# Block 0's weight and softmax steps taken off GpSimd, its list of steps made anew, and operand tiles padded to one address modulo 256 bytes

## The chip, the cores and the metric

The kernel runs on one core of one Trainium2 chip. A core has five engines with a queue of instructions each: TensorE (PE; its loads of stationary operands are shown apart as PEld), VectorE (DVE), ScalarE (ACT), GpSimd (POOL) and SyncE (SP), which only starts transfers here. Engines run beside each other and wait for each other by semaphores. The metric is the device time of one execution in microseconds, the median of the runs shown.

## The reference, cut to what matters

```python
# q, k, v: (8 batches, 8 heads, 576 tokens, 64), float32
scores = (q @ k.T) / sqrt(64)
# heads 0..3: local mask, 0 <= i - j < 32; heads 4..7: strided mask, j <= i and j % 32 == i % 32
attn = exp(scores - max) / (sum + 1e-9)
x = (attn @ v)                       # as (4608 tokens, 512)
gate = 1 / (1 + exp(-(x @ w_gate)))  # w_gate, w_val: (512, 1536), w_out: (1536, 512), float64
out = ((gate * (x @ w_val)) @ w_out).astype(float32)
```

Attention is sparse: a query of a local head sees 32 keys, a query of a strided head at most 18. Most arithmetic is in the three dense products of the gated layer, 4608 tokens by 512 by 1536.

## The kernel before, in words

**Precision.** The weights are float64 and TensorE works here on a 32-bit form (fp32r) that keeps part of the fraction. So every operand is held as two tiles, a high part and a low part (value less high part), and each dense product is issued three times: high by high, high by low, low by high. The twelve slices of the hidden dimension (f = 0 to 11) have three weights each (i = 0 gate, 1 value, 2 out); "w0_1" is slice 0's value weight. A weight reaches TensorE by seven steps: `wr` loads its 64-bit words; `wa` (L244) and `wb` (L248) turn the upper and the lower words into two tiles on ScalarE; `ws` (L252) shifts the upper on VectorE; `wd` (L256) adds the two, which gives the number in single precision; `wu` (L260) casts it to the high part; `wl` (L263) subtracts for the low part. `wd` and `wl` run on VectorE, their variants `wdp` and `wlp` on GpSimd; `wu` runs on ScalarE, its variant `wuv` on VectorE.

**Blocks.** Tokens are worked in blocks of 512: block k (0 to 7) holds the first 512 tokens of batch k, block 8 the 64 left over of each batch. For a block and a slice f, gate and value are 12 products of 512 columns each (L512: 4 pieces of the 512 inputs, 3 products each), then come the sigmoid (`s`, L520, ScalarE), gate times value (`m`, L525, VectorE), the split into hh (`x`, L532, ScalarE; variant `xv` on VectorE) and hl (`y`, L536, VectorE; variant `yp` on GpSimd), and 12 products with the out weight (`o`, L543), which add into four banks. In blocks 0 to 2 gate and value are done so. Blocks 3 and 4, 5 and 6, 7 and 8 are worked in pairs, where half products (L770) of sums and differences of weights (made on GpSimd during blocks 0 to 2, L693 to L698, and kept in DRAM) replace them; `ring` tiles bring those weights back, `xs` tiles hold sums of x.

**Attention.** Each batch is four pairs of heads (0 and 2 local, 1 and 3 strided). A pair of batches 0 and 1 goes through load (`fQ`, `fV`), scores on TensorE (`fS`, L329), mask (`fM`), row maximum (`fA`, L353), subtraction (`fU`, L357; variant `fUp` on GpSimd), exponential (`fE`, L370, ScalarE), sum and reciprocal (`fN`, L374 to L376), multiplication (`fW`, L380; variant `fWp` on GpSimd), transposes on TensorE (`fT`), a copy to pt (`fP`), the product with v on TensorE (`fX`, L433), and the split into xh (`fH`, L469), xl (`fL`, L473) and leftovers (`fR`, L482). While block 0 is in work, the weights arrive for the first time, and batch 1's attention is done between its products.

**What sets the order.** The list ORDER names every step of the program; a program walks it and issues each step's instructions, and no scheduler moves them. So the queue of each engine is the list with the other engines' steps left out, and an instruction whose operand is late holds all behind it on its engine. `fg0.1.2` is block 0's product of slice 0, weight 1 (value), third piece of x; `wu2.0` casts weight w2_0; a p behind the letters means GpSimd, a v VectorE. BANKS says which PSUM banks some of the first steps use.

**Addresses.** Tiles come from pools ("keep", "work", "first", "odd"), where each tag takes a place of its own size behind the others; so the size of one tile moves all that lie behind it. The tiles whose size the change touches are qk (an attention pair's q and k, L283) and mx (row maxima and sums, L308).

Of the kernel before, what the change touches and what calls it, by code (L numbers as in the profile page):

```python
# [73 lines left out]
wuv2.0 fg0.1.1 fH0.3 ws1.1 wlp2.0 wu1.0 fg0.0.1 fL0.3 wb1.1 fg0.1.2 wl1.0 fR0.3 wr3.2 wb0.2 fg0.0.2 wd1.1 wa0.2 fg1.0.0 wuv1.1 wa2.1 wr4.0 fg0.0.3
wl1.1 wb2.1 ws0.2 fg1.0.1 wr4.2 ws2.1 wdp0.2 fg1.1.0 wd2.1 fg0.1.3 s0.0 wuv2.1 wu0.2 fg1.1.1 m0.0 fg2.0.0 wl0.2 x0.0 fS1.0 wl2.1 wb3.0 yp0.0 wa1.2
wb1.2 fg1.0.2 fM1.0 fQ1.1 wa3.0 fg2.1.0 wr5.0 fA1.0 wb2.2 wr5.2 fg1.1.2 wa2.2 fU1.0 fg2.0.1 wr5.1 ws3.0 fg1.0.3 wd3.0 fg1.1.3 s0.1 ws1.2 fg2.0.2 wu3.0
m0.1 wlp3.0 fg2.1.1 xv0.1 fg2.0.3 wd1.2 fE1.0 fg2.1.2 yp0.1 wuv1.2 o0.0 fN1.0 wlp1.2 s0.2 fW1.0 wa3.1 wb3.1 ws3.1 wa4.1 ws2.2 fg3.0 wdp3.1 wr6.0 wa3.2
ws4.1 wb3.2 ws3.2 wd2.2 wu3.1 wr6.1 wdp3.2 wl3.1 wu2.2 fT1.0 wb4.1 wa4.0 wd4.1 wr7.0 fg2.1.3 fP1.0 fZ1.1 wuv4.1 wlp2.2 wb4.0 o0.1 m0.2 wr6.2 wuv3.2
s0.3 ws4.0 wlp3.2 x0.2 wa4.2 y0.2 wb4.2 fg3.1 ws4.2 wlp4.1 wr7.1 wd4.2 wuv4.2 wb5.1 wl4.2 fS1.1 wb5.2 m0.3 wa5.2 xv0.3 wa5.1 o0.2 fM1.1 fQ1.2 wr8.1
wr8.0 fA1.1 y0.3 fUp1.1 wd4.0 fX1.0 ws5.1 wu4.0 ws5.2 wlp4.0 o0.3 wd5.1 fR1.0 fV1.1 wdp5.2 fE1.1 fH1.0 fN1.1 wa5.0 fg4.0 wb5.0 fL1.0 fWp1.1 wu5.1  # L80
wr7.2 ws5.0 wu5.2 wd5.0 fg4.1 wl5.2 wlp5.1 s0.4 wu5.0 wa6.1 wl5.0 ws6.1 wb6.0 fT1.1 m0.4 wa6.0 xv0.4 wb6.1 fg5.0 y0.4 fP1.1 ws6.0 wb6.2 wd6.0 wa6.2
wuv6.0 wl6.0 fS1.2 wd6.1 s0.5 wa7.0 ws6.2 wdp6.2 fg6.0 wu6.1 fM1.2 fQ1.3 wb7.0 fA1.2 wl6.1 fUp1.2 ws7.0 wb7.1 fg5.1 wuv6.2 wa7.1 wl6.2 wdp7.0 ws7.1
wd7.1 fE1.2 fX1.1 wu7.1 m0.5 fN1.2 fg6.1 fV1.2 s0.6 wuv7.0 fWp1.2 x0.5 wl7.0 fH1.1 wl7.1 fR1.1 yp0.5 fL1.1 fg7.0 wa8.1 wb8.1 ws8.1 wa8.0 wr9.0 wdp8.1
m0.6 wa7.2 xv0.6 wb7.2 o0.4 y0.6 s0.7 ws8.0 wb8.0 ws7.2 wuv8.1 wr8.2 wlp8.1 fg7.1 wdp8.0 wdp7.2 wu8.0 fT1.2 m0.7 wl8.0 x0.7 o0.5 wuv7.2 fZ1.3 wb9.0
y0.7 fP1.2 wl7.2 wa9.0 wa8.2 ws9.0 wr9.2 wb8.2 wd9.0 fg8.1 wr9.1 wuv9.0 ws8.2 wlp9.0 wdp8.2 fS1.3 wuv8.2 o0.6 fM1.3 LQ0 wlp8.2 wa9.1 wb9.1 ws9.1 fA1.3
# [856 lines left out]
```

## Time and profile before

| | before |
|---|---|
| time, median of 3 runs (lowest to highest) | 956.06 us (954.44 to 957.01) |
| the profiled execution's own time | 955.16 us |
| its span, instructions | 953.4 us, 18540 |
| PE busy | 929.7 us, 98% |
| PEld busy | 757.6 us, 79% |
| DVE busy | 608.6 us, 64% |
| ACT busy | 418.6 us, 44% |
| POOL busy | 180.7 us, 19% |
| moved by DMA | 154.14 MB, 162 GB/s |

The span runs from the first to the last instruction of one profiled execution; the time of that execution is 1.8 us longer. A share is busy time over the span, so it is an average over stages with different limits. Instructions are named by their source line, the tile that they write and those that they read ("g<-xh,w"). Matmul ends are modelled, and a product of 512 columns is shown with about 390 ns although products follow each other faster than that, so the pace is to be read from starts of products, not from the sum of durations.

### The profile page before, as it was taken

What the parts mean: (1) busy time and instruction counts of PE and PEld (TensorE: products, weight loads), DVE (VectorE), ACT (ScalarE), POOL (GpSimd) and SP (SyncE); (2) the same over time, 40 slices, a digit from 0 to 9 for tenths busy, and PEclk for the clock granted to TensorE, in tenths of its full rate; (3) what the DMA queues carried; (4) which work ended last, traced back from release to release, by engine and by line L of the source; (5) the groups of instructions that cost most, each with busy time, mean ns of one, the idle gap of its engine ahead of it and who ended that gap; (6) DMA issues with size and microseconds to landing.
All of it is one profiled execution on the core that took longest, in us unless ns stands there. A gap on an engine that the chain in (4) does not pass through costs nothing.

```text
span 953.4 us, 18540 instructions
## 1 busy us (share of the span) xinstructions
PE 929.7 (98%) x7624; PEld 757.6 (79%) x7624; DVE 608.6 (64%) x973; ACT 418.6 (44%) x759; POOL 180.7 (19%) x226
## 2 busy tenths in 40 slices
PE   5988999999999999999999999999999999999998
...
GB/s 366 313 194 81 169 96 176 119 176 197 197 121 222 232 160 189 210 185 187 173 187 175 174 68 172 194 186 144 147 163 143 23 140 193 152 147 144 64 45 44
DMA packets 90068, 154.14 MB, mean 162 GB/s; under 512 B 5888, under 2 KB 40192, under 8 KB 89984
## 3 DMA queue, kind: packets, MB, share of 16 engines
...
q8 instruction: 60, 0.98, 0.4%
...
## 4 chain that ended last, share of the span: by engine, by line
PE 85%; DVE 8%; DMA 2%; ACT 2%; SPq 1%; issue 1%; POOL 1%; DVEq 0%; ACTq 0%
PE p L770 21%; PE o L543 18%; PE d L770 15%; PE g L512 7%; PE v L512 7%; PE o_a L543 5%; PE o_g L543 3%; PE o_v L543 3%; PE x_a L433 2%; DVE high L256 1%; DVE w L263 1%; PE s_g L329 1%; PE s_v L329 1%; PE s L329 1%; PE x L433 1%
## 5 line engine op out<-in xcount | busy, mean ns | idle before, releaser
L770 PE MATMUL p<-xs,ring 128*128 128x512 f32 x864 | 204.8, 389 | 0.0
L770 PEld LDWEIGHTS p<-xs,ring 128*128 128x128 f32 x864 | 162.2, 188 | 34.1
L543 PE MATMUL o<-w,hh 128*128 128x512 f32 x576 | 183.4, 399 | 0.0
L770 PE MATMUL d<-xs,ring 128*128 128x512 f32 x648 | 155.8, 389 | 0.0
L770 PEld LDWEIGHTS d<-xs,ring 128*128 128x128 f32 x648 | 121.6, 188 | 25.2
L543 PEld LDWEIGHTS o<-w,hh 128*128 128x128 f32 x576 | 106.4, 188 | 24.9
L543 PE MATMUL o<-w,hl 128*128 128x512 f32 x288 | 113.6, 395 | 0.0
L804 DVE TENSOR_TENSOR e<-e,d 128x512 f32<-128x512 f32 x54 | 37.1, 687 | 110.4 <-PE d L770 63.3
L401 DVE STREAM_TRANSPOSE pt<-sb 32x320 f32<-32x320 f32 (+1 forms) x192 | 102.9, 536 | 3.8
L512 PE MATMUL v<-xh,w 128*128 128x512 f32 x256 | 87.8, 400 | 4.6 <-DVE t L525 2.4
L512 PE MATMUL g<-xh,w 128*128 128x512 f32 x256 | 86.7, 396 | 2.8 <-DVE sb L349 1.2
L799 ACT COPY e<-p 128x512 f32<-128x512 f32 x54 | 31.7, 588 | 118.5 <-PE p L770 118.2
L543 PEld LDWEIGHTS o<-w,hl 128*128 128x128 f32 x288 | 54.2, 188 | 12.8
L512 PEld LDWEIGHTS v<-xh,w 128*128 128x128 f32 x256 | 49.0, 192 | 16.1 <-issue 2.8
L512 PEld LDWEIGHTS g<-xh,w 128*128 128x128 f32 x256 | 48.0, 188 | 15.5 <-DVE sb L349 1.8
L698 POOL TENSOR_TENSOR sum<-sum 128x128 f32<-128x128 f32 x96 | 51.2, 536 | 6.3
L536 DVE TENSOR_TENSOR hl<-hid,hh 128x512 fp32r<-128x512 f32 x36 | 28.0, 780 | 36.5 <-ACT hh L532 36.4
L512 PE MATMUL v<-xl,w 128*128 128x512 f32 x128 | 51.0, 399 | 0.0
L512 PE MATMUL g<-xl,w 128*128 128x512 f32 x128 | 50.2, 392 | 0.0
L693 POOL TENSOR_TENSOR sum<-w 128x256 f32<-128x256 f32 x44 | 34.9, 812 | 71.1 <-DMA sets<-sum 68.6
L812 ACT ACTIVATE e<-e 128x512 f32<-128x512 f32 x54 | 34.2, 633 | 28.7 <-DVE e L804 28.4
L532 ACT CAST hh<-hid 128x512 fp32r<-128x512 f32 x36 | 22.3, 620 | 53.0 <-PE o_a L543 43.6
...
## 6 DMA issues: line engine op xcount, KB each, us to landing
...
```

The lines of the kernel that those rows point to most:

```text
L329: nc.tensor.matmul(sc[j % len(sc)][g * m : (g + 1) * m, j // len(sc) * BANK + s * kk : j // len(sc) * BANK + (s + 1) * kk], q_[d, at : at ...
L401: nc.vector.transpose(dst[to : to + LB, :, col : col + LB], src[part * LB : (part + 1) * LB, :, h * LB : (h + 1) * LB])
L433: nc.tensor.matmul(at_bank(r, (u * per + g) * m, (u * per + g + 1) * m)[j * D : (j + 1) * D], v[part][rows, slot * P + j * D : slot * P + ...
L512: nc.tensor.matmul(o, w, x, start=first and n == 0, stop=last and n == len(todo) - 1)
L536: by.tensor_tensor(hl, whole_h.pop((k, f)), hh.bitcast(F32), op=ALU.subtract)
L543: nc.tensor.matmul(acc[k][i], h[:, i * P : (i + 1) * P], w, start=f == 0 and n == 0, stop=f == NF - 1 and n == 2,)
L693: nc.gpsimd.tensor_tensor(u[:, at : at + 2], part(wh[f][i], c), part(wl[f][i], c), op=ALU.add)
L698: nc.gpsimd.tensor_tensor(u[:, to], u[:, x], u[:, y], op=op)
L770: nc.tensor.matmul(to, w[:, (wi * 2 + c) * P : (wi * 2 + c + 1) * P], x[xi][:, c], start=p in (1, 2, 5) and c == j == 0, stop=c == 1 and j ...
L799: nc.scalar.copy(x, two[m, 0])
L804: nc.vector.tensor_tensor(x, x, two[m, 1], op=ALU.add)
L812: nc.scalar.activation(x, x, AF.Sigmoid)
```

## The change

It has three parts.

1. **Steps that change engine.** In the stretch of the list that builds block 0 (up to block 1's first gate), all variants on GpSimd go: 16 `wdp`, 13 `wlp`, 5 `yp`, 6 `fUp` and 4 `fWp` become `wd`, `wl`, `y`, `fU` and `fW` on VectorE. The variants of casts on VectorE go too: 21 `wuv` and 5 `xv` become `wu` and `x` on ScalarE.
2. **The list made anew.** That stretch, and the first steps behind it, stand in another order; 2329 steps before and after, the last 1703 the same and in the same order. BANKS gives some first steps other banks.
3. **Sizes of tiles.** The qk tile grows from 1198 to 1216 words (4792 to 4864 bytes in each partition, 19 times 256), and the mx tile from 16 to 64 words (64 to 256 bytes). The two pairs of batch 0 that borrow the places of weights (HOMES) share one kept tile mxs of 64 words in place of a tile of their own each.

The diff, with the list cut to its first lines:

```diff
@@ -36,6 +36,7 @@
 SK = NG * GS + QB - GS
 SQK = SK + NG * GS
+WIDE = 64 * -(-SQK // 64)
 TB = 512
@@ -54,7 +55,7 @@
 BANKS = {
-    "S0.0": "o1", "S0.1": "o1", "T0.1": "o0", "X0.1": "o0", "T0.2": "o1", "X0.2": "o1", "S0.3": "o1", "T0.3": "o0", "g1": "o0",
+    "T0.0": "o0", "X0.0": "o0", "S0.1": "o0", "T0.1": "o1", "X0.1": "o1", "T0.2": "o0", "T0.3": "o0", "X0.3": "o0", "g1": "o0",
 }
@@ -67,105 +68,105 @@
-fQ0.1 fZ0.1 fZ0.3 C fQ0.0 fQ0.2 fV0.2 fQ0.3 fV0.1 wr0.1 fV0.0 wr0.0 fS0.1 fV0.3 wr2.0 wr1.0 wr1.1 wr0.2 fM0.1 wr2.1 wr1.2 fA0.1 fS0.0 fU0.1 fQ1.0
-fM0.0 fE0.1 fS0.2 fN0.1 fA0.0 fW0.1 fUp0.0 fM0.2 fT0.1 fA0.2 fE0.0 fS0.3 fUp0.2 fP0.1 fN0.0 fX0.1 fM0.3 fWp0.0 fE0.2 fA0.3 fR0.1 fH0.1 fN0.2 wa0.1
-fUp0.3 fT0.0 wb0.1 fW0.2 wr3.0 fP0.0 fL0.1 fT0.2 fE0.3 ws0.1 wa0.0 fN0.3 wdp0.1 fX0.0 fP0.2 wb0.0 fW0.3 wu0.1 wr2.2 fX0.2 fV1.0 ws0.0 fR0.0 fH0.0
...
+fQ0.0 fZ0.1 fZ0.3 C fQ0.2 fQ0.1 fV0.0 fQ0.3 fV0.2 fV0.1 wr0.0 fV0.3 fS0.0 wr1.0 wr0.1 wr1.1 fM0.0 fQ1.0 wr2.0 wr2.1 fA0.0 wr0.2 fS0.2 wr1.2 fU0.0
+fE0.0 fM0.2 fS0.1 fN0.0 fA0.2 fM0.1 fU0.2 fS0.3 fW0.0 fE0.2 fA0.1 fT0.0 fN0.2 fP0.0 fW0.2 fU0.1 fT0.2 fM0.3 fE0.1 fN0.1 fP0.2 wa0.0 fX0.2 wb0.0 fW0.1
+wr2.2 fA0.3 fT0.1 fH0.2 wa1.0 fU0.3 fR0.2 fX0.0 fL0.2 fE0.3 ws0.0 fP0.1 fN0.3 fR0.0 fV1.0 fH0.0 fX0.1 wa0.1 fW0.3 wb0.1 fL0.0 fH0.1 wr3.0 wd0.0 fT0.3
...
@@ -182,6 +183,7 @@
     ident = cst[:, SL * KL + GS :]
+    mxs = pool.tile([P, 64], F32, name="mxs")
     xr = {}
@@ -280,7 +282,7 @@
-            qk = space.tile([P, SQK], F32, tag="qk", name=f"qk{b}_{step}")
+            qk = space.tile([P, WIDE], F32, tag="qk", name=f"qk{b}_{step}")
@@ -305,7 +307,7 @@
-            tiles["mx"] = space.tile([P, 16], F32, tag="mx" + str(step) * bool(home), name=f"mx{b}_{step}")
+            tiles["mx"] = mxs[:, 16 * step : 16 * step + 16] if home else space.tile([P, 64], F32, tag="mx", name=f"mx{b}_{step}")
```

Lines of the changed kernel stand two lower than those of the kernel before (L263 becomes L265).

Three places show what the new list does to the queues. The first is VectorE's queue around the first weights that are finished (w is the high and low part of one weight, high and low its two word tiles, xl the low part of batch 0's x, mx and sb an attention pair's row values and scores). Before:

```order
L380 TENSOR_TENSOR sb0_3_83<-sb0_3_83,mx0_3_84 128x12x54
L252 TENSOR_SCALAR high0_0_363<-high0_0_363 128x512
L256 ISA high0_0_363<-high0_0_363,low0_0_364 128x1024
L473 TENSOR_TENSOR xl0_74<-x0_0_370,xh0_73 128x512
L260 CAST w0_0_472<-high0_0_363 128x512
L263 TENSOR_TENSOR w0_0_472<-high0_0_363,w0_0_472 128x512
L252 TENSOR_SCALAR words2_0_460<-words2_0_460 128x512
L473 TENSOR_TENSOR xl0_74<-x0_2_416,xh0_73 128x512
L252 TENSOR_SCALAR high1_0_491<-high1_0_491 128x512
L256 ISA high1_0_491<-high1_0_491,low1_0_492 128x1024
L260 CAST w2_0_525<-words2_0_460 128x512
```

And with the change:

```order
L382 TENSOR_TENSOR sb0_3_84<-sb0_3_84,mxs_62 128x12x54
L475 TENSOR_TENSOR xl0_75<-x0_0_364,xh0_74 128x512
L258 ISA high0_0_306<-high0_0_306,low0_0_307 128x1024
L254 TENSOR_SCALAR high0_1_443<-high0_1_443 128x512
L254 TENSOR_SCALAR high1_0_359<-high1_0_359 128x512
L265 TENSOR_TENSOR w0_0_465<-high0_0_306,w0_0_465 128x512
L258 ISA high0_1_443<-high0_1_443,low0_1_444 128x1024
L475 TENSOR_TENSOR xl0_75<-x0_1_414,xh0_74 128x16x18
L475 TENSOR_TENSOR xl0_75<-x0_1_414,xh0_74 128x16x12
L475 TENSOR_TENSOR xl0_75<-x0_1_414,xh0_74 128x16x2
L265 TENSOR_TENSOR w0_1_520<-high0_1_443,w0_1_520 128x512
L258 ISA high1_0_359<-high1_0_359,low1_0_360 128x1024
```

The casts (L260) have left VectorE; the adds and subtractions of w0_1, GpSimd's before, stand in the queue, and between the steps of one weight stand steps of another.

The second place is GpSimd's queue from the program's branch on (sum tiles are the sums of weights for the later blocks). Before:

```order
L938 UNCONDITIONAL_BRANCH
L310 MEMSET sb0_1_80 128x12x10
L310 MEMSET sb0_3_83 128x12x10
L357 ISA
L357 TENSOR_TENSOR sb0_0_195<-sb0_0_195,mx0_0_196 128x640
L357 TENSOR_TENSOR sb0_2_246<-sb0_2_246,mx0_2_247 128x640
L380 TENSOR_TENSOR sb0_0_195<-sb0_0_195,mx0_0_196 128x640
L357 TENSOR_TENSOR sb0_3_83<-sb0_3_83,mx0_3_84 128x12x54
L256 TENSOR_TENSOR high0_1_333<-high0_1_333,low0_1_334 128x512
L263 TENSOR_TENSOR w0_1_412<-high0_1_333,w0_1_412 128x512
L256 TENSOR_TENSOR words2_0_460<-words2_0_460 128x512
L263 TENSOR_TENSOR w2_0_525<-words2_0_460,w2_0_525 128x512
```

With the change:

```order
L940 UNCONDITIONAL_BRANCH
L312 MEMSET sb0_1_81 128x12x10
L312 MEMSET sb0_3_84 128x12x10
L312 MEMSET sb1_1_689 128x12x10
L312 MEMSET sb1_3_1364 128x12x10
L695 ISA
L695 TENSOR_TENSOR sum0_0_1_1777<-w0_0_465 128x256
```

Until the first sum of weights GpSimd now only sets four tiles to zero.

The third place is TensorE's queue around block 0's first gated product (t are transposes, x attention results, v and g products of the value and the gate weight). Before:

```order
L433 MATMUL x0_0_370<-pt0_0_348,vv0_0_105 64x32 x36
L433 MATMUL x0_2_416<-pt0_2_407,v0_2_93 64x32 x32
L433 MATMUL x0_2_416<-pt0_2_407,u0_2_95 64x32 x4
L388 MATMUL t0_3_462<-cst_61,sb0_3_83 128x128 x6
L512 MATMUL v0_0_478<-xh0_73,w0_1_412 128x512
L512 MATMUL v0_0_478<-xl0_74,w0_1_412 128x512
L512 MATMUL v0_0_478<-xh0_73,w0_1_412 128x512
L512 MATMUL g0_0_486<-xh0_73,w0_0_472 128x512
```

With the change:

```order
L435 MATMUL x0_0_364<-pt0_0_285,vv0_0_93 64x32 x36
L435 MATMUL x0_1_414<-pt0_1_404,vv0_1_103 64x54 x22
L390 MATMUL t0_3_455<-cst_61,sb0_3_84 128x128 x6
L331 MATMUL s1_0_472<-qk1_0_159 32x64 x40
L514 MATMUL g0_0_522<-xh0_74,w0_0_465 128x512
L514 MATMUL g0_0_522<-xl0_75,w0_0_465 128x512
L514 MATMUL g0_0_522<-xh0_74,w0_0_465 128x512
L435 MATMUL x0_3_530<-pt0_3_513,v0_3_107 64x54 x22
```

The gate's weight comes first instead of the value's, and the scores of batch 1's first pair have moved ahead of the first gated product.

More of the change, by code (lines that the diff above doesn't have):

```diff
@@ L74 @@
[L74 to L85, printed above, removed]
@@ new lines @@
+fg1.1.1 ws2.0 fE1.0 fg0.1.3 wr4.0 wd2.0 fg1.0.1 fN1.0 wu2.0 fg0.0.3 wb1.2 fg1.1.2 ws2.1 fW1.0 fg1.0.2 wd2.1 s0.0 fg1.1.3 wu2.1 m0.0 fg1.0.3 wb3.0
+wl2.0 fT1.0 s0.1 wl2.1 x0.0 ws0.2 fg2.0.0 y0.0 fP1.0 fZ1.1 wa1.2 fg2.1.0 m0.1 wr5.0 fg2.0.1 wd0.2 x0.1 fX1.0 wu0.2 y0.1 wa3.0 wl0.2 wr5.2 ws1.2
+fg2.1.1 fH1.0 fV1.1 ws3.0 fR1.0 fg2.0.2 wb3.1 fL1.0 wa3.1 fg2.1.2 wd1.2 ws3.1 wr6.0 o0.0 wu1.2 wd3.1 wa2.2 wl1.2 wu3.1 wd3.0 wb3.2 wl3.1 wu3.0 fg2.1.3
+wb2.2 wl3.0 fg2.0.3 wa4.1 wr5.1 ws2.2 fS1.1 wd2.2 s0.2 wu2.2 m0.2 o0.1 fM1.1 fQ1.2 x0.2 wb4.0 fA1.1 wa3.2 wa4.0 wr6.1 fU1.1 wr6.2 fg3.0 y0.2 wl2.2
@@ new lines @@
+y1.6 B2.3 g1.7 pw1.1.0 Z3 pw1.1.1 pd1.1.0 pd1.1.1 v1.7 s1.7 g1.8 m1.7 pa2.0.0 x1.7 y1.7 pa2.0.1 pl2 v1.8 s1.8 pb2.0.0 pb2.0.1 ph2.0.0.1 o1.6 m1.8
+pw2.0.0 x1.8 pd2.0.0 y1.8 ph2.0.1.0 pw2.0.1 X2.0 pd2.0.1 S3.0 LV3 H2 R2 L2 o1.7 LQ4 M3.0 pa2.1.0 M3.1 D3 A3 U3 pa2.1.1 g1.9 E3 pb2.1.0 N3 v1.9 W3 s1.9
+pb2.1.1 ph2.1.0.1 B3.0 B3.1 ph2.1.1.0 o1.8 m1.9 B3.2 x1.9 y1.9 g1.10 B3.3 pw2.1.0 pw2.1.1 pd2.1.0 v1.10 pd2.1.1 s1.10 g1.11 m1.10 pa3.0.0 x1.10 y1.10
+pa3.0.1 v1.11 pl3 s1.11 pb3.0.0 o1.9 m1.11 pb3.0.1 ph3.0.0.0 x1.11 pw3.0.0 y1.11 pd3.0.0 X3.0 S4.0 LV4 H3 R3 o1.10 L3 LQ5 M4.0 pa3.1.0 M4.1 D4
@@ new lines @@
+U13 V3.1.1 c3.1.0.1 E13 G3.1.2 N13 r11 c3.1.1.1 V3.1.2 ad3.1.0.2 W13 sg3.1.2 G3.1.6 r12 ad3.1.1.2 B13.0 V3.1.6 c3.1.0.6 B13.1 G3.1.5 r13 c3.1.1.6
+B13.2 V3.1.5 B13.3 G3.1.7 mu3.1.2 x3.2 V3.1.7 y3.2 c3.1.0.7 ad3.1.0.7 G3.1.4 r14 c3.1.1.7 sg3.1.7 ad3.1.1.7 V3.1.4 sg3.1.4 mu3.1.7 G3.1.3 r15 mu3.1.4
+x3.3 V3.1.3 ad3.1.0.3 y3.3 sg3.1.3 o3.1 r16 ad3.1.1.3 mu3.1.3 X13.0 S14.0 LV14 H13 R13 o3.2 LQ15 M14.0 M14.1 A14 D14 U14 G3.2.1 E14 N14 V3.2.1
+c3.2.0.1 W14 G3.2.2 r17 c3.2.1.1 B14.0 V3.2.2 ad3.2.0.2 B14.1 sg3.2.2 G3.2.6 r18 ad3.2.1.2 B14.2 V3.2.6 c3.2.0.6 B14.3 G3.2.5 c3.2.1.6 mu3.2.2 Z15
@@ new lines @@
+mu5.4.4 x5.9 V5.4.3 ad5.4.0.3 y5.9 sg5.4.3 o5.7 ad5.4.1.3 mu5.4.3 o5.8 G5.5.1 V5.5.1 c5.5.0.1 G5.5.2 r69 c5.5.1.1 xh7.0.1 xh7.1.1 V5.5.2 xl7.0.1
+ad5.5.0.2 xl7.1.1 G5.5.6 sg5.5.2 r70 ad5.5.1.2 xh7.0.2 xh7.1.2 mu5.5.2 V5.5.6 c5.5.0.6 xl7.0.2 x5.10 xl7.1.2 G5.5.5 r71 c5.5.1.6 y5.10 V5.5.5 G5.5.7
+r72 V5.5.7 c5.5.0.7 ad5.5.0.7 G5.5.4 r73 c5.5.1.7 sg5.5.7 ad5.5.1.7 V5.5.4 sg5.5.4 mu5.5.7 G5.5.3 mu5.5.4 x5.11 V5.5.3 y5.11 ad5.5.0.3 o5.9 r74
+ad5.5.1.3 sg5.5.3 xh7.0.3 mu5.5.3 xh7.1.3 xl7.0.3 xd7.0.0 xl7.1.3 o5.10 x6.0 xd7.0.1 xh7.0.5 y6.0 xh7.0.6 xl7.0.5 xl7.0.6 xd7.0.2 o5.11 x6.1 e5.0 y6.1
@@ new lines @@
+c7.2.0.7 ad7.2.0.7 G7.2.4 r90 c7.2.1.7 sg7.2.7 ad7.2.1.7 V7.2.4 sg7.2.4 mu7.2.7 G7.2.3 r91 mu7.2.4 x7.5 V7.2.3 ad7.2.0.3 y7.5 sg7.2.3 o7.3 r92
+ad7.2.1.3 mu7.2.3 o7.4 G7.3.1 V7.3.1 c7.3.0.1 G7.3.2 r93 c7.3.1.1 V7.3.2 ad7.3.0.2 sg7.3.2 G7.3.6 ad7.3.1.2 mu7.3.2 V7.3.6 c7.3.0.6 x7.6 G7.3.5 y7.6
+r94 c7.3.1.6 V7.3.5 G7.3.7 r95 V7.3.7 c7.3.0.7 ad7.3.0.7 G7.3.4 r96 c7.3.1.7 sg7.3.7 ad7.3.1.7 V7.3.4 sg7.3.4 mu7.3.7 G7.3.3 r97 mu7.3.4 x7.7 V7.3.3
+ad7.3.0.3 y7.7 sg7.3.3 o7.5 r98 ad7.3.1.3 mu7.3.3 o7.6 G7.4.1 V7.4.1 c7.4.0.1 G7.4.2 c7.4.1.1 V7.4.2 ad7.4.0.2 sg7.4.2 G7.4.6 r99 ad7.4.1.2 mu7.4.2
```

160 lines of the change are left out of this document (76 added, 84 removed).

## The prediction

> **What bounds the kernel now.** I read the page first (engine totals, slices), then the stretches by stage, the waits of PE, and last the pace of single products. Engine totals, and the slices of PE and of its clock:
>
> ```profile
> span 953.4 us, 18540 instructions
> PE 929.7 (98%) x7624; PEld 757.6 (79%) x7624; DVE 608.6 (64%) x973; ACT 418.6 (44%) x759; POOL 180.7 (19%) x226
> ...
> PE   5988999999999999999999999999999999999998
> ```
>
> TensorE is the bound everywhere but in the first four slices (96 us). So a gain has two sources: fewer PE gaps in block 0, or a quicker product. Stretches, columns: stretch, length, busy us (x instructions) of PE, PEld, DVE, ACT, POOL, then granted clock, DMA share, GB/s:
>
> ```profile
> 0.00:147.20 147.20, 131.19 (x1445) 105.37 (x1446) 118.59 (x190) 92.01 (x172) 67.52 (x61) 0.99 0.58 200
> ...
> 30.00:100.00 70.00, 64.96 (x617) 51.35 (x610) 65.05 (x99) 52.96 (x94) 32.19 (x23) 0.98 0.53 171
> ...
> 100.00:130.00 30.00, 30.00 (x243) 24.14 (x242) 22.48 (x39) 18.01 (x30) 15.82 (x13) 1.00 0.60 191
> ...
> 60.00:70.00 10.00, 10.00 (x147) 7.67 (x147) 9.73 (x15) 4.00 (x8) 3.70 (x3) 0.85 0.69 228
> ```
>
> 147.2 us is where block 1's first product starts. Until 100 us DVE is busy 93% of the time: it feeds PE, and PE waits for it. From 60 to 70 us the granted clock is 0.85, a loss of 1.5 us, right behind the longest wait. The waits of PE up to 250 us, then the rows where block 0 starts, where its first gated product starts, and where block 1 starts:
>
> ```profile
> PE v L512 <- DVE t L525: 2.4, 1, 2.4
> PE v L512 <- ACT w L260: 2.2, 1, 2.2
> ...
> PE g L512 <- DVE h L260: 0.6, 1, 0.6
> PE g L512 <- ACT e L520: 0.5, 1, 0.5
> ```
> ```profile
> 4.63 1.54 PE L329 MATMUL s<-qk 64*64 64x54 f32 x48 [4.63 <-DMA qk<-in_qk_s]
> ...
> 6.24 0.90 DVE L349 TENSOR_TENSOR sb<-s,cst 128x324 f32<-128x324 f32 x2 [6.24 <-PE s L329]
> ...
> 27.58 0.77 PE L512 MATMUL v<-xh,w 128*128 128x512 f32 x1
> ...
> 147.18 0.40 PE L512 MATMUL g<-xh,w 128*128 128x512 f32 x1
> ```
>
> So block 0 loses 5.7 us to four waits and 1.5 us to the clock after its first product.
>
> **Part 1: the addresses.** Each product of 512 columns loads 128 stationary columns and streams 512. Before, w, ring, xs and the even blocks' xh, xl start at 96 modulo 256 bytes, and hh, hl, xh1 and xl1 at 224; after, all at 96. Stretches show what that costs (L543: w against hh, hl; L770: xs against ring; L512 first in block 1, xh1 and xl1, then in block 2, xh and xl; columns: stretch, length, busy us and count of that line's products, clock, DMA, GB/s):
>
> ```profile
> 720.00:770.00 50.00, 42.00 (x180) 1.00 0.23 81
> ...
> 148.00:954.00 806.00, 282.38 (x1164) 217.35 (x1164) 1.00 0.49 154
> ```
> ```profile
> 860.00:885.00 25.00, 19.22 (x84) 1.00 0.45 145
> ```
> ```profile
> 211.80:223.50 11.70, 11.36 (x48) 1.00 0.64 203
> 328.70:340.00 11.30, 11.09 (x48) 1.00 0.63 187
> ```
>
> The first and the last three are unbroken runs (the second row counts L543 after 148 us, and has PEld behind PE), so (busy − 0.39 us, the last product's own duration) / (count − 1) is the step from one product to the next: the unbroken L543 run 41.61/179 = 232.5 ns; L770 18.83/83 = 226.9 ns; L512 in block 1 10.97/47 = 233.4 ns, in block 2 10.70/47 = 227.7 ns. The last pair decides: same line, same weights, same shape, only the address of x differs. A mismatch costs 5.6 ns. After 147.2 us there are 1164 products of L543 (second row), 264 of L512 with xh1 or xl1 against w (12 gates and 12 values of 12 products, less weight 11, which lies at 224 beside them), and 24 of block 2 against weight 11: 1452 x 5.6 ns = **−8.1 us**. Block 0 has 132 of L543 ahead of block 1's first product and 24 against weight 11: 156 x 5.6 = −0.9 us, counted below.
>
> The Trainium skill speaks against this term: TensorE: Matmul & The Clock Gate, section Step-by-step: what each phase is for, says that PE reads the moving operand and the next weights through two independent read ports, so that loading takes nothing from a running product. By it the address would not matter and the term would be 0; the two L512 rows above say otherwise, and I go by them.
>
> The attention's small products also change partner: pt moves from 224 to 96 under vv at 96. In local pairs half of the offsets gain what the other half loses; strided pairs of batches 2 to 7 now match, 484 records in the page's terms, at most 5.6 ns each: 0 to −2.7 us; I take 0, since weight loads space them. The wider qk tile and the shared mx add no instruction.
>
> **Part 2: block 0's steps off GpSimd.** GpSimd loses 44 instructions up to block 1, VectorE gains them and passes 26 casts to ScalarE. What GpSimd's work does to VectorE (groups in the first 150 us: count, busy us, mean ns; the first four meet GpSimd's work often, the next four hardly):
>
> ```profile
> L256 DVE CUSTOM_DVE_ANT_0 high<-high,low 128x1024 uint16<-128x1024 uint16 x18 | 18.2, 1013 | 0.9
> L252 DVE TENSOR_SCALAR high<-high 128x512 int32<-128x512 int32 x30 | 17.4, 591 | 3.4 <-ACT high L244 3.4
> L263 DVE TENSOR_TENSOR w<-high,w 128x512 fp32r<-128x512 f32 x18 | 17.4, 973 | 1.4 <-ACT w L260 1.1
> ...
> L532 DVE CAST hh<-t 128x512 fp32r<-128x512 f32 x5 | 4.2, 841 | 0.2
> ...
> L252 DVE TENSOR_SCALAR words<-words 128x512 int32<-128x512 int32 x6 | 2.5, 419 | 0.0
> ...
> L263 DVE TENSOR_TENSOR l<-high,h 128x512 fp32r<-128x512 f32 x2 | 1.4, 692 | 0.1
> L256 DVE CUSTOM_DVE_ANT_0 words<-words 128x1024 uint16<-128x1024 uint16 x2 | 1.4, 685 | 0.0
> L260 DVE CAST w<-words 128x512 fp32r<-128x512 f32 x3 | 1.3, 422 | 0.0
> ```
> ```profile
> 10.54 0.17 DVE L375 TENSOR_SCALAR mx<-mx 128x12 f32<-128x12 f32 x1
> ...
> 35.27 1.41 POOL L256 TENSOR_TENSOR words<-words 128x512 int32<-128x512 int32 x1 [2.75 <-DVE words L252]
> ...
> 35.66 1.56 DVE L256 CUSTOM_DVE_ANT_0 high<-high,low 128x1024 uint16<-128x1024 uint16 x1
> ...
> 37.60 0.68 DVE L525 TENSOR_TENSOR t<-e,v 128x512 f32<-128x512 f32 x1
> ...
> 38.20 0.68 DVE L263 TENSOR_TENSOR w<-words,w 128x512 fp32r<-128x512 f32 x1
> ```
>
> A DVE add of 0.69 us took 1.56 us while GpSimd added: DVE stood until it was done. The excess of the first four groups is 18 x 0.33 + 30 x 0.17 + 18 x 0.28 + 5 x 0.42 = 18.2 us. Against it stand 34 instructions of 0.69 us and 10 of 0.83 us added (31.8 us) and 26 casts of 0.42 us gone (10.9 us): 31.8 − 10.9 − 18.2 = +2.7 us on 118.6. DVE's load stays, but its instructions no longer wait in turn for a slow neighbour. The rows at 37.60 and 38.20 also show that independent instructions follow each other 0.60 us apart, 0.08 us less than one lasts; in the new list nearly all neighbours are independent. ScalarE takes 26 casts and two table loads fewer:
>
> ```profile
> L520 ACT ACT_TABLE_LOAD x5 | 6.4, 1283 | 0.1
> ...
> L260 ACT CAST w<-words 128x512 fp32r<-128x512 f32 x3 | 1.8, 614 | 1.1 <-POOL words L256 1.1
> ```
>
> 26 x 0.61 − 2 x 1.28 = +13.4 us on 92.0 of 147: room is left, so its count costs nothing; what could cost is VectorE waiting for it in turn.
>
> *First product.* In the new list VectorE has ahead of the first finished weight (w0_0): four softmaxes, two low parts of x, three shifts, one add, one subtract. Attention rows:
>
> ```profile
> L374 DVE TENSOR_REDUCE mx<-sb 128x12 f32<-128x648 f32 x4 | 3.3, 824 | 1.7 <-ACT sb L370 1.6
> L344 DVE TENSOR_TENSOR sb<-s,cst 128x640 f32<-128x640 f32 x4 | 3.3, 818 | 0.0
> ...
> L473 DVE TENSOR_TENSOR xl<-x,xh 128x512 fp32r<-128x512 f32 x4 | 2.7, 686 | 0.0
> ...
> L380 DVE TENSOR_TENSOR sb<-sb,mx 128x648 f32<-128x648 f32 x2 | 1.7, 827 | 0.0
> ...
> L376 DVE RECIPROCAL mx<-mx 128x12 f32<-128x12 f32 x4 | 0.9, 228 | 0.1
> ```
>
> Per softmax 0.82 to 0.90 (mask; the row at 6.24) + 0.82 (max, as long as the sum) + 0.83 (subtract, as long as the multiply) + 0.82 + 0.17 + 0.23 (sum, guard at 10.54, reciprocal) + 0.83 = 4.6 us; four and the rest, 1.4 + 1.3 + 0.7 + 0.7, make 22.5 us; less 0.08 for each of some 20 independent neighbours, 20.9 us. From 6.24 us on that is 27.1 us. Walking both queues in order adds 2.7 us of waits, an estimate: for the fourth exponential, for xh of pair 0, and 1 us for w0_0's high part, which on ScalarE stands behind xh of pair 1. First product at 29.8 us, 2.3 later than before; but the scores of batch 1 (1.0 us of PE, later before) are done by then: **+1.3 us**.
>
> *After it.* I summed VectorE's work and PE's work ahead of each product along the new list. VectorE's lead over PE's own work is 10.4 us at the first product, 11.4 at weight 2 (its highest, **+1.0 us** of PE waiting), 9.4 at weight 4, 9.0 at weight 5, 6.5 at batch 1's third transposes. So from weight 2 on VectorE has 2 to 5 us in hand. The four waits (−5.7) and the clock's fall (−1.5) go where VectorE keeps this; new waits stand against them, bounded by VectorE's idle share over its 62 us of work between the first product and that transpose: 0 at no idle; at 7% (its share from 30 to 100 us) 62/0.93 − 62 = 4.7, less 4.9 in hand, about 0 to 1; at 25% (its share from 100 to 130 us, when it was not needed) 20.7 − 4.9 = 15.8. The 7% row is the nearest, being of the same busy stage; I take **1.5 us**. With −0.9 of addresses, block 0: +1.3 + 1.0 − 7.2 + 1.5 − 0.9 = **−4.3 us**.
>
> **Sum.** The profiled execution took 955.16 us (span 953.4). 955.16 − 8.1 − 4.3 = 942.8. The median of the three runs, 956.06, lies 0.9 above it: **943.6 us**.
>
> **Rivals.**
> *VectorE starves PE.* Work that ran beside it now stands in its queue, and each weight passes ScalarE, VectorE, ScalarE, VectorE. For it: 93% busy already. Against it: the lead falls from weight 2 on, and GpSimd's stalls are gone. At 14% idle 62/0.86 − 62 = 10.1, less 4.9 = 5.2 us; at 20%, 15.5 − 4.9 = 10.6: 947 to 953, say 950. Chance 0.18.
> *The pace is not the address's.* Then 232.5 ns belongs to L543 (a weight streamed, four banks in turn), and block 1's rows to something I don't see: 943.6 + 9.0 = 952.6, and about 950 if block 0 gains more. For it: L543 has no matched run of its own. Against it: the two L512 rows. Chance 0.07.
> *Slower: PE's clock falls again and again.* A wait of 2.4 us was followed by 1.5 us lost, so such a wait costs 3.9. Place: PE's products of weights 2 to 7 waiting for VectorE. Three such waits give 955.3, no change; from the fourth on it is slower: 959.2. Against it: PE's new waits should be near 1 us. Chance 0.05. The page of the Trainium skill named above, section What's actually happening, has the clock fall only after an idle window of about 3.4 us; by that no wait foreseen here would cost clock and this rival's chance would be nearly 0, but the 0.85 stood behind 2.4 us.
>
> **How the numbers follow.** The forecast, 938 to 947, has 0.65; below it, if VectorE never idles and the small products match too, 0.05 (943.6 − 1.5 − 2.7 = 939.4 and less); the rivals 0.18, 0.07, 0.05. The range 937 to 952 leaves out the slow rival, the upper end of the first and a little below. A change under 0.3% (2.9 us) can't be told from none. Faster (under 953.2): 0.65 + 0.05 + 0.07 + most of 0.18 = 0.91; within: 0.05; slower: 0.04.
>
> **What would show it.** Addresses: the 180 products of L543's runs in 41.2 instead of 42.0 us, and block 1's L512 at 227 ns; else part 1 is wrong. Block 0: first product near 30 us, DVE's adds at 0.69 us throughout, block 1's first product near 143 us, no clock below 1 from 60 to 70 us. If PE's waits for DVE or ACT sum to over 5 us, or block 1 starts after 147 us, part 2 is wrong.

## The result, and the profile after

The changed kernel takes 940.66 us in the median of four runs (939.46 to 941.29), the kernel before 956.35 in the runs beside it: a ratio of 0.9838, 95% interval 0.982 to 0.9856, or 15.7 us less. The forecast was 943.6 us (937 to 952), 12.4 less. The profiled execution after took 939.46 us. Totals and PE's slices of its page:

```profile
span 937.7 us, 18515 instructions
...
PE 918.2 (98%) x7624; PEld 756.4 (81%) x7624; DVE 606.4 (65%) x991; ACT 430.8 (46%) x783; POOL 119.8 (13%) x182
...
PE   5999999999999999999999999999999999999998
```

Only the first slice of 23 us and, as before, the last still show TensorE idle. The starts of block 0's first gated product, of block 1 and of block 2 in the timeline of TensorE after, and block 2's before (27.58 and 147.18 stand in the prediction):

```profile
30.39 0.80 PE L514 MATMUL g<-xh,w 128*128 128x512 f32 x1
...
139.20 0.39 PE L514 MATMUL g<-xh,w 128*128 128x512 f32 x1
...
247.53 0.39 PE L514 MATMUL g<-xh,w 128*128 128x512 f32 x1
```
```profile
257.92 0.40 PE L512 MATMUL g<-xh,w 128*128 128x512 f32 x1
```

| stretch | before, us | after, us | difference |
|---|---|---|---|
| to the first gated product | 27.58 | 30.39 | +2.8 |
| from there to block 1 | 119.60 | 108.81 | −10.8 |
| block 1 | 110.74 | 108.33 | −2.4 |
| block 2 to the end of the span | 695.5 | 690.2 | −5.3 |

So 8.0 us come from block 0 and 7.7 from all that follows, where the list of steps is the same but for its first part.

**Behind block 0** the products whose two operands lay apart before are quicker by a little. The unbroken run of 180 out products (stretch, length, busy and count, clock, DMA), and a run of 48 gate and value products in block 1, after:

```profile
710.00:760.00 50.00, 40.96 (x180) 1.00 0.23 80
...
202.00:213.70 11.70, 11.04 (x48) 1.00 0.62 202
```

(40.96 − 0.39)/179 = 226.6 ns a step, where 42.00 us gave 232.5; (11.04 − 0.39)/47 = 226.6 ns in block 1, where 11.36 gave 233.4.

**In block 0** TensorE waits for nothing from the first gated product on. Its waits up to 250 us, and stretches (columns as in the prediction's):

```profile
PE s L331 <- DMA qk<-in_qk_l: 4.8, 1, 4.8
PE s L331 <- DMA k<-in_qk_s: 3.1, 1, 3.1
PE s L331 <- DMA k<-in_qk_l: 1.5, 1, 1.5
...
PE g L514 <- DVE sb L346: 0.6, 1, 0.6
...
```
```profile
30.39:139.20 108.81, 108.81 (x900) 88.55 (x897) 92.54 (x169) 90.52 (x166) 0.70 (x3) 1.00 0.55 178
30.00:100.00 70.00, 70.00 (x607) 56.71 (x589) 64.30 (x120) 63.36 (x117) 0.62 (x2) 1.00 0.58 188
...
60.00:70.00 10.00, 10.00 (x49) 8.32 (x48) 9.15 (x18) 8.78 (x15) 0.00 (x0) 1.00 0.69 226
```

All waits but the 0.6, which is in block 1, stand before 30.39 us. PE is busy for all of the 70 us in which it had lost 5 us, and the clock of 0.85 from 60 to 70 us is 1.00. VectorE is as busy as before there (64.3 against 65.1 us), with 120 instructions in place of 99. Its groups in the first 150 us after:

```profile
L258 DVE CUSTOM_DVE_ANT_0 high<-high,low 128x1024 uint16<-128x1024 uint16 x30 | 20.5, 688 | 1.4 <-ACT low L250 0.5
L265 DVE TENSOR_TENSOR w<-high,w 128x512 fp32r<-128x512 f32 x28 | 19.1, 689 | 4.0 <-ACT w L262 2.8 <-DMA sets<-w 0.7
L254 DVE TENSOR_SCALAR high<-high 128x512 int32<-128x512 int32 x30 | 12.5, 421 | 4.4 <-ACT high L246 3.9
L538 DVE TENSOR_TENSOR hl<-t,hh 128x512 fp32r<-128x512 f32 x12 | 8.4, 699 | 1.2 <-ACT hh L534 1.0
```

30 adds take 20.5 us where 18 took 18.2 (0.69 against 1.01 us each), 28 subtractions 19.1 where 18 took 17.4, 30 shifts 12.5 in place of 17.4.

### The profile page after: what moved, and what is told of

Its sections match the earlier page's. It is cut to its first block, busy times and chain, and to the rows that moved or that the text cites. A ratio compares the mean times of both kernels' runs of the same rounds, so it can differ in the third digit from the quotient of the medians.

```text
span 937.7 us, 18515 instructions
## 1 busy us (share of the span) xinstructions
PE 918.2 (98%) x7624; PEld 756.4 (81%) x7624; DVE 606.4 (65%) x991; ACT 430.8 (46%) x783; POOL 119.8 (13%) x182
## 4 chain that ended last, share of the span: by engine, by line
PE 93%; DVE 3%; DMA 2%; ACT 1%; POOL 0%; SPq 0%; issue 0%; DVEq 0%
PE p L772 21%; PE o L545 20%; PE d L772 16%; PE g L514 9%; PE v L514 9%; PE o_a L545 5%; PE o_g L545 3%; PE o_v L545 3%; PE x_a L435 2%; PE x L435 1%; DMA k<-in_qk_s 1%; PE s_g L331 1%; PE s_v L331 1%; DVE pt L403 1%; PE t L390 1%; PE s L331 1%
## 5 line engine op out<-in xcount | busy, mean ns | idle before, releaser
L545 PE MATMUL o<-w,hh 128*128 128x512 f32 x576 | 180.5, 395 | 0.0
L514 PE MATMUL v<-xh,w 128*128 128x512 f32 x256 | 85.5, 391 | 0.0
```

Of the source, the lines that this page charges most:

```text
L514: nc.tensor.matmul(o, w, x, start=first and n == 0, stop=last and n == len(todo) - 1)
L545: nc.tensor.matmul(acc[k][i], h[:, i * P : (i + 1) * P], w, start=f == 0 and n == 0, stop=f == NF - 1 and n == 2,)
```

## The experiments

Two theories were to be told apart for each part. For the sizes: the pace belongs to the operands' addresses, or to the kind of product or the list. For block 0: the moved engines make the gain, or the new order, or only both.

### The sizes alone, and the list alone

The first kernel is the one before with `WIDE`, the mx of 64 words and mxs, its own list and banks; the second is the one before with the change's list and banks, its own sizes.

```diff
 # sizes alone
+WIDE = 64 * -(-SQK // 64)
+    mxs = pool.tile([P, 64], F32, name="mxs")
-            qk = space.tile([P, SQK], F32, tag="qk", name=f"qk{b}_{step}")
+            qk = space.tile([P, WIDE], F32, tag="qk", name=f"qk{b}_{step}")
 ...
```

> The kernel before with the new tile sizes alone (qk 1216 words, mx 64 words, the kept mxs); list, engines and banks as before. Theory (a product whose two operands differ modulo 256 bytes takes 5.6 ns more; 1608 such products): 9.0 us less than before, about 947.3 us; L543's products step by 227 ns instead of 232; block 0 keeps PE's four waits (5.7 us) and its clock of 0.85 from 60 to 70 us. Rival (the pace belongs to L543's kind of product or to the list): within 1 us of before, 956, L543 still at 232 ns.

> The kernel before with the new list and banks (so the steps on VectorE and ScalarE), and the tile sizes of before. Theory (the two parts add): 15.7 us gained in all less 8.6 to 9.0 for the addresses leaves 6.7 to 7.1: about 949.3 us; L543's products step by 232 ns throughout; block 1 starts 0.9 us later than with both parts, at about 140 us. Rival (the new list alone makes the gain): about 941, products at 227 ns.

Measured: the sizes alone 947.67 us (ratio 0.991, 0.9895 to 0.9925), 8.7 less than the 956.34 beside it; the list alone 948.59 (0.9922, 0.9907 to 0.9937), 7.75 less. Together they would make 16.4; the change made 15.7. The same 180 out products, of the sizes alone and then of the list alone:

```profile
715.00:765.00 50.00, 40.96 (x180) 1.00 0.22 77
```
```profile
715.00:765.00 50.00, 42.00 (x180) 1.00 0.22 74
```

With the old list and the new sizes they take 40.96 us, as after; with the new list and the old sizes 42.00, as before. So the pace follows the sizes and nothing in the list. What follows block 1's start is 798.4 us with the sizes alone and 806.1 with the list alone (806.2 before, 798.5 after). Block 0 keeps its waits with the sizes alone:

```profile
PE v L514 <- DVE t L527: 2.5, 1, 2.5
PE v L514 <- ACT w L262: 2.2, 1, 2.2
...
```

Its block 1 starts at 146.49 us, 0.7 sooner than before; with the list alone it starts at 140.99, 6.2 sooner.

### Which addresses are quick

hh, the stationary operand of two products in three of an out step, is shifted inside a wider tile, by another number of words for each slice f. To make room, the row values of the two borrowed pairs lie behind their scores.

```diff
-        hs[k, f] = [work.tile([P, TB], F32R, tag=n, name=f"{n}{k}_{f}", bufs=3) for n in ("hh", "hl")]
+        at = (0, 32, 16, 8, 4, 2, 1, 48, 24, 40, 56, 64)[f]
+        hh = work.tile([P, TB + 64], F32R, tag="hh", name=f"hh{k}_{f}", bufs=3)[:, at : at + TB]
+        hs[k, f] = [hh, work.tile([P, TB], F32R, tag="hl", name=f"hl{k}_{f}", bufs=3)]
```

> The change, with hh (the stationary operand in two thirds of L545's products) shifted inside a wider tile by 0, 128, 64, 32, 16, 8, 4, 192, 96, 160, 224 and 256 bytes for the slices 0 to 11; hl, the weights and all else stay at 96 modulo 256 (row values of the two borrowed pairs lie behind their scores, which frees the room). The step from one product with hh to the next, by slice. Theory A (only equality modulo 256 bytes is quick): 227 ns for slices 0 and 11, 232 for the ten others. Theory B (the cost grows with the distance on the circle of 256 bytes): 232 at 128 bytes, half of it near 64 and 192, nothing at 4 to 16. Theory C (which half of a 256-byte stretch the address is in): 232 where 96 plus the shift passes 128 (32, 64, 96, 128), 227 for the others. Products with hl: 227 throughout. By A the whole takes 720 x 5.6 ns = 4 us more than the change.

> The first table of shifts again with other shifts: hh starts 16, 48, 80, 112, 144, 176, 208, 240, 128, 8, 64 and 0 bytes behind 96 modulo 256 for the slices 0 to 11. In the first table products with hh at equal addresses stepped by 227 ns, at 16 bytes by 228, at the nine others by 230 to 234. Theory A (only equality modulo 256 is quick, 16 bytes an exception of that slice): slice 11 at 227, all others 230 to 234, the 16 bytes of slice 0 among them. Theory D (odd multiples of 16 bytes are quick too): slices 0 to 7 near 228, slices 8 to 10 at 231 to 234.

In these kernels the out products stand in L546. Block 6 issues its slices one after the other, 12 products each, so a stretch from one slice's first product to the next slice's, divided by 12, is the step. Slices 0, 1 and 4 of the first table (shifts 0, 128 and 16 bytes; the thirteenth product counted is the one still running at the start), then slice 0 of the second (16):

```profile
724.35:727.08 2.73, 2.73 (x13) 1.00 0.51 192
727.08:729.88 2.80, 2.80 (x13) 1.00 0.10 39
...
735.46:738.21 2.75, 2.75 (x13) 1.00 0.01 3
```
```profile
724.70:727.43 2.73, 2.73 (x13) 1.00 0.51 192
```

| hh's shift, bytes | 0 | 4 | 8 | 16 | 32 | 48 | 64 | 80 | 96 | 112 | 128 | 144 | 160 | 176 | 192 | 208 |
|---|---|---|---|---|---|---|---|---|---|---|---|---|---|---|---|---|
| ns a step in block 6 | 227 | 232 | 231, 233 | 227, 229 | 232 | 231 | 233 | 233 | 230 | 231 | 233, 234 | 233 | 231 | 230 | 232 | 231 |

The table holds both kernels, from the same starts with one digit more. Slices 10 and 11 are not in it, since their products alternate in block 6. Nearly every shift costs 3 to 7 ns, a shift of 4 bytes as much as one of 192. So it is not the distance (B) nor the half of the 256 bytes (C), and odd multiples of 16 are not quick as such (D falls at 48, 80, 112, 176 and 208). Theory A holds in the main, and slice 11 of the first table, shifted by 256, is quick too (226.7 ns in blocks 0 and 1). One thing was expected wrongly: products with hl, whose address was equal, did not keep 227 ns. So the weights of the next product count, and not only a product's own.

The address alone does not decide it, though. The second table's slice 7 (240 bytes) has the same weights and the same shift in every block; the first two rows are its 12 steps in block 5 and in block 6. The next two are slice 11 of that table in block 7, whose shift is 0 and which follows slice 10 with a shift of 64: its first six steps and its last six.

```profile
691.83:694.55 2.72, 2.72 (x12) 1.00 0.28 106
744.12:746.92 2.80, 2.80 (x14) 1.00 0.02 6
902.87:904.26 1.39, 1.39 (x8) 1.00 0.00 0
904.26:905.61 1.35, 1.35 (x7) 1.00 0.02 6
```

Slice 7 takes 227 ns a step in block 5 and 233 in block 6. Slice 11, at equal addresses, takes 231 at first and 226 to 227 after six products. So what ran before counts as well. 16 bytes (0 to 2 ns), 240 bytes, and 144 in block 0 (226.6 ns) are the exceptions, and why is open. The whole took 944.93 and 945.36 us, in one run each, 4.3 and 4.7 more than the change, against 4 expected.

### Engines and order apart

Both kernels have the new sizes. The first has the old list with the 70 steps renamed to their new engines at their old places, the second the new list with the steps back on their old engines.

```diff
 # engines changed, old order
-fM0.0 fE0.1 fS0.2 fN0.1 fA0.0 fW0.1 fUp0.0 fM0.2 ...
+fM0.0 fE0.1 fS0.2 fN0.1 fA0.0 fW0.1 fU0.0 fM0.2 ...
 # new order, old engines
-wr2.2 fA0.3 fT0.1 fH0.2 wa1.0 fU0.3 ...
+wr2.2 fA0.3 fT0.1 fH0.2 wa1.0 fUp0.3 ...
```

> The new tile sizes and the 44 steps on VectorE and 26 casts on ScalarE, but each at its old place in the list and with the old banks. Theory A (engines and order both count: old places were spaced for three engines side by side): no DVE instruction is stretched any more (adds at 0.69 us), but VectorE and ScalarE wait for each other in turn; PE's waits in block 0 stay at 4 to 12 us, time 946 to 954. Theory B (the stalls that GpSimd causes are the whole matter, the order nothing): about 941, as the change. Theory C (moving without reordering is a loss against the sizes alone): above 949.

> The change's list with the 44 steps back on GpSimd and the 26 casts back on VectorE, at their new places; new tile sizes and banks. Theory A (GpSimd's work stretches VectorE's and is itself slow, 1.4 us for an add): VectorE's adds are again 1.0 us in the mean in block 0, PE waits in block 0 for 5 to 15 us, time 946 to 956. Theory B (the order is the whole matter, the engines nothing): about 941.

| sizes as after; time, and block 1's start | old engines | new engines |
|---|---|---|
| old order | 947.67, 146.49 | 946.69, 145.93 |
| new order | 952.31, 152.06 | 940.66, 139.20 |

Neither half is worth anything alone. Moving the steps at their old places gains 1.0 us, within the intervals (0.9888 to 0.9918 against 0.9895 to 0.9925); the new order with the old engines loses 4.6. That order was made for the new engines, so this does not show what another order would do for the old ones. In the kernel with moved engines in the old order VectorE's adds are as short as after, but VectorE stands idle for its partner:

```profile
L258 DVE CUSTOM_DVE_ANT_0 high<-high,low 128x1024 uint16<-128x1024 uint16 x30 | 20.3, 686 | 0.7
L265 DVE TENSOR_TENSOR w<-high,w 128x512 fp32r<-128x512 f32 x28 | 18.9, 685 | 7.9 <-ACT w L262 7.8
```

Before its subtractions it waits 7.8 us for ScalarE's casts of the weights (2.8 after): the steps of one weight stand one behind the other there, and the hand-overs are waited for. PE's own waits there between 32 and 147 us are 2.8 us, less than the 4 to 12 expected, and they are for ScalarE:

```profile
PE g L514 <- ACT e L522: 2.3, 2, 1.2
PE s L331 <- ACT pt L411: 0.5, 1, 0.5
```

How VectorE's idle time leads to these is argued from the queues and not shown. With the new order on the old engines the links are slow instead. PE's waits there between 32 and 147 us, and a group each of GpSimd and of VectorE:

```profile
PE g L514 <- ACT e L522: 3.0, 2, 2.4
PE t L390 <- POOL sb L382: 2.6, 1, 2.6
...
PE g L514 <- POOL w L265: 0.8, 1, 0.8
```
```profile
L258 POOL TENSOR_TENSOR high<-high,low 128x512 int32<-128x512 int32 x12 | 15.9, 1332 | 19.5 <-DVE high L254 9.3 <-ACT xh L471 6.1 <-ACT low L250 4.2
```
```profile
L538 DVE TENSOR_TENSOR hl<-t,hh 128x512 fp32r<-128x512 f32 x6 | 6.9, 1152 | 1.1 <-ACT hh L534 1.0
```

An add takes 1.33 us on GpSimd, against 0.69 on VectorE in the change, and VectorE's subtraction for hl, 0.70 after, takes 1.15 beside it. VectorE's own adds were expected at 1.0 us and take 0.73. PE's waits come to 8.6 us.

### GpSimd's work without its chain

The change, with three adds on GpSimd at each of the 44 old places, into a tile that nothing reads.

```diff
+    def beside():
+        for _ in range(3):
+            nc.gpsimd.tensor_tensor(idle, ident, ident, op=ALU.add)
```

> The change, with three adds of 128 columns on GpSimd (0.5 us each, of the constant identity into a tile that nothing reads) at each of the 44 places where the list of before had a GpSimd step: 132 adds, about 66 us of GpSimd, that no step waits for. Theory A (GpSimd's work stretches VectorE's beside it): VectorE's adds (L258 there: their line) go from 0.69 to 0.9 us and more in the mean in block 0, VectorE falls behind, PE waits for it and block 1's first product moves from 139.2 to 143 us or later; the time rises to 944 to 952. Theory B (GpSimd's old steps cost only by being slow links in the chain to PE): VectorE's durations rise little and the time stays at 940 to 942.

Measured: 946.04 us (0.9888, 0.9875 to 0.9902), 5.4 more than the change; block 1 starts at 146.52, 7.3 later. VectorE's first groups:

```profile
L260 DVE CUSTOM_DVE_ANT_0 high<-high,low 128x1024 uint16<-128x1024 uint16 x30 | 22.5, 754 | 1.4 <-ACT low L252 0.7
L267 DVE TENSOR_TENSOR w<-high,w 128x512 fp32r<-128x512 f32 x28 | 21.3, 773 | 3.3 <-ACT w L264 2.2 <-DMA sets<-w 0.7
L256 DVE TENSOR_SCALAR high<-high 128x512 int32<-128x512 int32 x30 | 15.1, 510 | 3.8 <-ACT high L248 3.6
L540 DVE TENSOR_TENSOR hl<-t,hh 128x512 fp32r<-128x512 f32 x12 | 9.8, 817 | 0.8 <-ACT hh L536 0.7
```

Theory A holds in kind, though the stretch is smaller than it said (0.75 in place of 0.9 us); these adds last 0.58 us each, the old ones 1.33. The four groups take 8.2 us more than after. Of block 1's 7.3 us, 5.6 arise behind the first gated product, where PE waits 4.3 us; the other 1.7 are a first product at 32.13 us. Work on GpSimd that nobody waits for is not free beside a full VectorE.

### The casts back on VectorE

```diff
-wuv to wu, xv to x (26 casts, ScalarE)
+wuv, xv (VectorE), at the places of the new list
```

> The change with only the 26 casts (21 of weights, 5 of hh) back on VectorE, at their new places; the 44 steps stay on VectorE too, GpSimd stays empty in block 0. VectorE gets 26 x 0.42 = 10.9 us more; between the first gated product and block 1 it was busy 92.5 of 108.8 us in the change, from 30 to 100 us 64.3 of 70. Theory A (VectorE is full where it counts, from 30 to 100 us): about 18 casts fall there, 7.6 us against 5.7 us idle; PE waits for VectorE, block 1 starts 2 to 8 us later than 139.2, time 943 to 949. Theory B (VectorE's idle time takes them, since a cast on VectorE needs no hand-over to ScalarE and back): block 1 within 1 us of 139.2, time 940 to 942.

Measured: 942.61 us (0.9863, 0.9847 to 0.988), 1.95 more than the change (the two intervals overlap, but all four runs lie above all of the change's), block 1 at 142.59. VectorE from 30 to 100 us, and PE's waits from 32 to 147 us:

```profile
30.00:100.00 70.00, 69.61 (x642) 55.72 (x636) 66.21 (x129) 53.39 (x99) 0.20 (x1) 1.00 0.58 185
```
```profile
PE t L390 <- DVE sb L382: 1.1, 1, 1.1
PE g L514 <- ACT e L522: 0.4, 1, 0.4
```

This lies between the two theories. VectorE takes most of the casts in its idle time (66.2 of 70 us busy in place of 64.3), and PE waits 1.5 us, most of it (1.1) just behind that stretch. Of block 1's 3.4 us, 2.5 arise behind the first gated product; the other 0.9 are a first product at 31.24 us, which in the profiles of kernels with the change's list lies anywhere from 30.0 to 31.8.

### A version that goes further

Two waits of 0.6 us for VectorE's mask are left in blocks 1 and 2, and VectorE's queue of softmax work was thought to set the first product. The first kernel cuts two out steps in halves. In the next two TensorE, idle then, adds the mask of two pairs of batch 0 to their scores; the scores of one of them take another bank.

```diff
-... s1.0 pb0.0.0 pl0 o0.11 m1.0 x1.0 e0.0 y1.0 d0.0 e0.1 S0.0 d0.1 LQ1 M0.0 M0.1 D0 g1.1 ...
+... s1.0 pb0.0.0 pl0 oh0.11.0 m1.0 x1.0 e0.0 y1.0 d0.0 e0.1 S0.0 oh0.11.1 d0.1 LQ1 M0.0 M0.1 D0 g1.1 ...
 # masks behind the scores, in score()
+                    nc.tensor.matmul(todo["soft"][0][:, j], ident, m_, start=False, stop=True, skip_group_check=True)
 # masks first
+                    nc.tensor.matmul(todo["soft"][0][:, j], ident, m_, start=True, stop=False, skip_group_check=True)
```

> The change, with two steps of out products (o0.11, o1.11) cut into two halves, the second half put behind the scores S0.0 and S5.0, where a gate's product waited 0.6 us for VectorE's mask. Theory (PE has nothing else to wait for there): the two waits go, 1.2 us less, 939.5. Rival: the half that comes later makes its readers late and the waits return behind it: 940.7.

> The kernel with the two splits, and for the pairs 1 and 2 of batch 0 the mask added to the scores by TensorE (identity times mask, into the same bank) in place of VectorE, which then reads maximum and subtraction from the bank. Theory A (up to the first gated product VectorE's queue sets the start): VectorE has 1.7 us less to do, less 0.1 for two subtractions cut in halves; the first gated product comes 1.5 us sooner than at 30.4, and as all of VectorE's later work moves with it, 1.5 us less in all: 938.0. Theory B (weights arrive too late, or TensorE's masks hold the scores back): first product at 30 us or later, no gain.

> As the kernel with masks by TensorE and the two splits, but with the mask laid into the bank first and the scores added to it. Theory A (VectorE's queue sets the start): as there, first gated product at about 29 us against 30.0 to 32.1 in the runs with the change's list, time 938.4. Theory B (the masks, now ahead of the scores in TensorE's queue, hold the first scores back): first product past 30 us, time 940 or more.

The splits alone: 940.38 us (0.9829, 0.9816 to 0.9843), no change that can be told from 940.66. Block 1 is 0.67 us shorter (107.66), as its wait is gone; in block 2 the wait for the mask is gone and one of 0.4 us for VectorE's transposes has come (690.24 us to the end against 690.14), which is the rival. With masks behind the scores: 938.43 us (0.9808, 0.9795 to 0.9822); the output comes out otherwise than the reference's that way (by 0.09, relative), so this one is read for its times alone. With the mask laid first: 938.38 us (0.9826, 0.9804 to 0.9849; four times 937.93, 938.02, 938.75 and 942.63). Its first gated product, and a stretch ahead of it:

```profile
29.04 0.80 PE L532 MATMUL g<-xh,w 128*128 128x512 f32 x1
```
```profile
17.59:31.24 13.65, 12.66 (x305) 0.50 1.02 400
```

The first product comes at 29.04 us, sooner than in any profile with the change's list (30.03 to 31.78), as theory A said. But VectorE's queue is not all that sets it. In the change's own profile, two pieces of the chain that ended last at the first product are a load and the scores that it released:

```profile
4.04 9.51 DMA k<-in_qk_s
...
13.69 1.54 PE s L331 x48
```

From there that chain runs mostly through TensorE. In the kernel with masks first it runs through VectorE from 10.87 to 16.95 us instead. Of the 1.35 us that the first product gains on the change's, block 1 keeps 0.6 (138.57 against 139.20). This version beats the kernel before; its median is 2.3 us under the change's, but the two intervals overlap, so that it beats the change is likely and not shown.

## Why the prediction was right, step by step

**Addresses.** 1608 products by 5.6 ns, 9.0 us, were forecast; the sizes alone gave 8.7 in the medians, and 7.8 of the 8.1 behind block 0. The two L512 rows on which the step rested were enough to tell it. The rule weighed there, that of the Trainium skill (TensorE: Matmul & The Clock Gate, section Step-by-step: what each phase is for), by which loading weights takes nothing from a running product, is not what these traces show: with the same list the 180 products take 42.00 or 40.96 us, by the sizes of two tiles alone.

**First product.** Forecast 29.8 us, measured 30.39. The scores of batch 1's first pair that moved ahead of it were taken as 1.0 us of PE, and so they are: from start to start, without waits, the scores' line takes 3.70 us for 256 products behind the first gated product before and 2.67 for 176 after. The net is +1.8 us in place of +1.3. That the start came so near is partly luck: the profiles with the change's list have it anywhere from 30.03 to 31.78, and the working walked the queues but not the loads.

**Behind it** the forecast was −7.2 for waits and clock, and +1.0 and +1.5 for new waits of PE on VectorE. This is where it was mis-sized: the two terms for new waits measured nothing. The working took VectorE's idle share as lost time; in the row from 30 to 100 us VectorE is idle for 5.7 us and PE for none, so its idle time fell where PE had work in hand. The casts brought back show how near the edge this is: with 1.9 us more of VectorE's work in that stretch, PE waits 0.4 us in it and 1.1 just behind.

**What went** was also larger than −7.2: at equal sizes the stretch from the first gated product to block 1 fell from 118.94 (27.55 to 146.49, the sizes alone) to 108.81 us, 10.1, of which 1.0 are the scores; 9.1 remain. The waits are 5.4 of it and eight products at 427 in place of 227 ns 1.6; some 2.1 us I cannot assign. So block 0 came to −8.0 in place of −4.3: 2.5 from new waits that did not come, 1.9 from this, less 0.5 at the first product and 0.2 of addresses.

**VectorE's load** was to rise by 2.7 us (18.2 us of stretch gone, 31.8 added, 10.9 taken off) on 118.6. Up to block 1 it fell to 113.5:

```profile
0.00:139.20 139.20, 128.01 (x1444) 104.88 (x1445) 113.53 (x206) 103.66 (x195) 1.24 (x9) 1.00 0.64 218
```

The durations after are those that the rows read beside an idle GpSimd gave (0.69, 0.42). But the sum of the stretch stopped at four groups. The casts were stretched too; in the first 150 us before, two of their groups were

```profile
L260 DVE CAST w<-high 128x512 fp32r<-128x512 f32 x16 | 7.6, 477 | 2.7 <-POOL high L256 2.4
...
L260 DVE CAST h<-high 128x512 fp32r<-128x512 f32 x2 | 1.9, 962 | 1.0 <-POOL high L256 1.0
```

and with hh's five (4.2) and the three others (1.3) the 26 took 15.0 us. The sum had 13.0 for them (10.9, and 2.1 of hh's excess), so this is 2.0 us of the 7.8 between forecast and measurement. 3.0 more lie in groups that it left out: the guard of the softmaxes (L375, 0.41 and 0.30 us each, 0.17 after), three subtractions of words (1.05, 0.69 after) and hl (0.75, 0.68 after). That VectorE had less to do than forecast may be a reason why the forecast waits did not come. But this balance is not the gain: with the same durations in the old order block 1 starts only 0.6 us sooner. The prediction named the order (neighbours that do not wait for each other) beside the stalls and gave the two one price; the experiments show that either without the other is worth nothing.

**The rivals.** VectorE starving PE did not come, but its conditions were near, as said. That the pace is not the address's fell with the sizes alone. The clock fell nowhere behind the first product; the section on the hardware says what that hangs on.
